# Two heads' attention scores as a pair of matmuls on the two halves of TensorE's rows, instead of one full-height matmul for each head

## The chip, the core and the metric

The kernel runs on one core of a Trainium2 chip. The metric is the device time of one execution in microseconds (us), the median of several runs. TensorE (PE) multiplies matrices and keeps its weights in a separate load (PEld), VectorE (DVE), ScalarE (ACT) and GpSimd (POOL) work on what it leaves in PSUM or on SBUF, and SyncE (SP) issues most of the DMAs.

## The reference

```python
xn = layernorm(x)                                   # x: 2048 x 576
qkv = (xn @ wqkv).reshape(B, S, 3, 32, 18)          # 32 heads of 18 numbers
scores = einsum("bhqd,bhkd->bhqk", q, k) * 18**-0.5
mask = (i - j >= 0) & (i - j < 256)                 # causal, a window of 256
p = softmax(where(mask, scores, -1e9))
s = einsum("bhqk,bhkd->bhqd", p, v).reshape(B, S, D) @ wo
z = gelu(xn @ w_in);  z1, z2 = z[:2304], layernorm(z[2304:])
g = w_sp @ z2 + b_sp                                # w_sp: 2048 x 2048
out = x + s * silu((z1 * g) @ w_out)
```

The change is in `scores` and in the row maxima that the softmax subtracts. Everything else stays as it is.

## The kernel before

Products are made in fp32r, each factor split into a high and a low part where precision asks for it. The kernel goes through these stages, told with the stretch of the profiled execution that they take: layernorm, q and k (stored to DRAM in `st_d` as high and low parts) and v (0 to 203 us); the z2 product (203 to 444 us, matmul line L688); a stage of heads, in which attention is computed and the z1 product (L460) is woven in as filler (444 to 940 us); then the large `w_sp` product in Strassen form (L1001), `wo` and `w_out` to the end.

**Attention.** The work is cut into 16 units: 4 heads and one half of the 2048 positions each. An SBUF tile `att` (a slot) holds two heads. A head's q takes 54 rows, high part, the same high part again, and low part, against k's low, high and high part, so that one matmul over 54 rows gives the whole product. Head 0 of a slot sits on rows 0 to 53, head 1 on rows 64 to 117. k of both heads shares the same columns, but q of the two heads stands in separate columns, and the other head's rows there are zero. A matmul for one head therefore reads all the rows of the slot, and the zeros take the other head out.

**Row maxima** (`row_max`, L398 on). For each head and each block of 128 queries a matmul `sp` (L409, 118 rows, 384 keys wide, 256 in the first two blocks) writes a PSUM tile of the pool `sps`, and DVE reduces it to a maximum in one custom instruction with an accumulator read behind it (L413). After 32 of these, a small transpose (`sp<-ident,mx`, L421) turns the maxima of the unit into rows, DVE splits them in two parts (L425, L426), and `put_max` (L428) sends them by two DMAs on POOL's queue into rows 126 and 127 of the slots, where k has ones. `row_max` is a generator. One `next` of it is a step: one matmul with its reduction, or one of three steps at the end (35 steps a unit).

**Scores for the softmax** (`scores`, L523 on). For each block of 128 keys and each head a matmul `tps` (L539, all 128 rows, so that the maximum is subtracted inside the product, 384 or 256 queries wide) writes a PSUM tile of the pool `tps`, and ACT takes the exponential out of it (L543). After four heads POOL masks the corners (L546, L549), and later `pv` (L552 on) multiplies by v: groups of four matmuls `ops` (L562), one head in each 32 columns of TensorE.

**PSUM.** All eight banks are taken: two each for `mm` (z1, z2), `sp`, `tps` and `ops`. So the pools `sps` and `tps` have two tiles each, and a matmul that wants a tile waits until DVE or ACT is done with the tile two before it.

**Order.** The stages with attention are under a manual schedule: the instructions of PE, DVE, ACT and POOL stand as the Python loops issue them, so the order of the code is the order on each engine. In the z2 stage two steps of `row_max` go into each group of 14 matmuls over its last blocks, to get ahead of the heads (L684 to L691; `RMN + LEAD` steps in all). In the heads' stage the loop over `items` (L745 on) takes one head of one key block at a time: its `tps` matmul, then alternately a filler (`fill`, one z1 matmul) and a step of `row_max` as they fall due, and every four key blocks a burst of `pv`. Loads of a head (`load_head`, four DMAs) and of v are issued at fixed items, two units ahead.

Of the kernel before, what the change touches and what calls it, by code (L numbers as in the profile page):

```python
# [9 lines left out]
F32 = mybir.dt.float32  # L10
# [6 lines left out]
P = 128  # L17
# [15 lines left out]
SLOT = 2 * HS + HS + 256  # L33
# [6 lines left out]
RMN = 35  # L40
LEAD = 16
# [4 lines left out]
DR = 118  # L46
LOAD_AT = (1, 9, 16, 24)
# [16 lines left out]
def kernel(  # L64
# [47 lines left out]
    dve.reduce_sum(low, ident[:64, :64].rearrange("p (a n b) -> p n a b", n=2, b=16)[:, 1], axis=mybir.AxisListType.XY)  # L112
# [133 lines left out]
    with ExitStack() as early:  # L246
# [103 lines left out]
        with ExitStack() as ph:  # L350
# [3 lines left out]
            def clear(i):  # L354
                eng = (dve, pool)[i % 2]
                eng.memset(f32(slots[i][:, 0:2 * HS]), 0.0)
                eng.memset(f32(slots[i][:, 2 * HS:]), 1.0)
# [3 lines left out]
            def q_of(u, j):  # L361
                t = slots[(2 * u + j // 2) % NSLOT]
                return t[:, (j % 2) * HS:(j % 2 + 1) * HS]

            def k_of(u, j):
                return slots[(2 * u + j // 2) % NSLOT][:, 2 * HS:]

            def load_head(u, j):
                g, half = UNITS[u]
                q0 = half * HS  # L370
                k0, kn = (0, HS) if half == 0 else (HS - 256, HS + 256)
                h = 4 * g + j
                q, k = f32(q_of(u, j)), f32(k_of(u, j))
                b = 64 * (j % 2)
                qs, ks = st_d[0, :, h, q0:q0 + HS], st_d[1, :, h, k0:k0 + kn]
                sp.dma_start(q[b:b + 36, :], qs)
                sp.dma_start(k[b:b + 18, :kn], ks[18:36])
                sp.dma_start(q[b + 36:b + 54, :], qs[18:36])
                sp.dma_start(k[b + 18:b + 54, :kn], ks)
# [18 lines left out]
            def row_max(u):  # L398
# [3 lines left out]
                for j in range(4):  # L402
                    for i in range(8):
                        qb = 8 * half + i
                        w = 384 if qb >= 2 else 256
                        k0 = (max(qb - 2, 0) - base) * P
                        m0 = {0: 256, 1: 128}.get(qb, 0)
                        ps = sps.tile([P, 384], F32, name="sp")
                        pe.matmul(ps[:, :w], q_of(u, j)[:DR, i * P:(i + 1) * P], k_of(u, j)[:DR, k0:k0 + w],  # L409
                                  start=True, stop=True)  # L410
                        spend(MM * w / 512 + 20)
                        junk = aa.tile([P, 384], mybir.dt.bfloat16, name="junk")
                        dve.tensor_tensor_reduce(out=junk[:, :w], in0=ps[:, :w], in1=band[:, m0:m0 + w], scale=1.0,  # L413
                                                 scalar=-3.0e38, op0=ALU.add, op1=ALU.max,
                                                 accum_out=mx[:, j // 2, 0, j % 2, i:i + 1])
                        yield
                dve.tensor_copy(mx[:, :, 1], mx[:, :, 0])
# [3 lines left out]
                pe.transpose(pt[:64, :P], mx.rearrange("p a n b i -> p (a n b i)"), ident)  # L421
# [6 lines left out]
                def put_max(n):  # L428
                    t = slots[(2 * u + n) % NSLOT]
                    pool.dma_start(f32(t[126:128, 0:2 * HS]), f32(m[32 * n:32 * n + 32, :]))  # L430

                for n in range(2):
                    after(1000 + 600 * n, partial(put_max, n))
# [89 lines left out]
            def scores(u, kb, qa, qz, j):  # L523
# [3 lines left out]
                if j == 0:  # L527
# [7 lines left out]
                if n == 1:  # L535
                    a = qa - 1 if qa > lo else qa
                m = max(n, 2)
                ps = tps.tile([P, 384], F32, name="tps")
                pe.matmul(ps[:, :m * P], k_of(u, j)[:, (kb - base) * P:(kb - base + 1) * P],  # L539
                          q_of(u, j)[:, (a - lo) * P:(a - lo + m) * P], start=True, stop=True)  # L540
                spend(MM * m / 4 + 20)
                d0 = (qa - kb) * P
                act.activation(pt[:, j, d0:d0 + n * P], ps[:, (qa - a) * P:(qa - a + n) * P], AF.Exp, scale=scale)  # L543
                if j == 3:
# [173 lines left out]
            with ExitStack() as heads:  # L718
# [22 lines left out]
                for u in range(NU):  # L741
# [3 lines left out]
                    items = [(s, j) for s in steps for j in range(4)]  # L745
                    heads_at = {LOAD_AT[i]: (u + 2, i) for i in range(4) if u or i > 1}
                    have, want = done, (total - TAIL) * WEIGHT[u]
                    for t, (s, j) in enumerate(items):
# [3 lines left out]
                        if u == NU - 1 and t == 4:  # L752
# [17 lines left out]
                        while z >= 0.5 or r >= 0.5:  # L770
                            if z >= 0.5:
                                fill(1)
                                z -= 1
                            if r >= 0.5:
                                next(stream, None)
                                maxed += 1
                                r -= 1
                            if z < 1.5 and j == 3 and len(todo) >= (PVN if u < NU - 1 else 2):
                                burst()
                        if j == 3 and len(todo) >= (PVN if u < NU - 1 else 2):  # L780
                            burst()
                        if j == 3:
                            todo.append((u, *s))
                        if j == 1:
                            extra(1)
                        if t == 12 and u + 1 < NU:
                            load_v(u + 1)
                        if u == NU - 1 and t >= 8 and prep:
                            prep.pop(0)()
# [426 lines left out]
```

## Time and profile before

| | |
|---|---|
| median of 3 runs | 1939.77 us (1939.09 to 1940.27) |
| the profiled execution | 1937.71 us |
| its span, first to last instruction | 1936.0 us |
| granted TensorE clock, mean | 0.999 |
| PE matmul busy | 1910.9 us (99%) |
| DVE / ACT / POOL busy | 1076.2 (56%) / 892.4 (46%) / 288.1 us (15%) |
| the same in 446 to 940 us (494 us) | PE 493.0, DVE 299.2, ACT 311.3, POOL 171.1 us |

A line such as `650.28 0.33 PE L539 MATMUL tps<-att 128*128 128x384 f32 x1` says: at 650.28 us of the span, 0.33 us long, on PE, from line 539 of the kernel, tile `tps` from tile `att`, 128 rows by 128 columns of weights, 384 numbers streamed. Matmuls are pipelined: what one costs is the distance from its start to the start of the next, and not its length, which holds the time until its result has landed. What stands in square brackets is how long the engine sat idle before and who released it; "issue" there means that the engine waited for nothing that the profile shows.

### The profile page before, as it was taken

How to read it: one execution, taken by the hardware profiler on the slowest of the kernel's cores; microseconds unless marked ns; L12 is line 12 of the kernel's file. 1: busy time of each engine (PE TensorE's matmuls, PEld its weight loads, DVE VectorE, ACT ScalarE, POOL GpSimd, SP SyncE). 2: the span in 40 equal slices, each digit the busy share in tenths (PEclk: the TensorE clock that was granted, in tenths of full speed). 3: DMA queues.
4: the chain of work that ended last, by engine and by line, in shares of the span. 5: the costliest groups of instructions: out<-in, count | busy, mean ns of one | idle time of the engine just before them, and what ended most of it. 6: DMA issues, size and time to landing. Idle time of an engine off the chain costs nothing.

```text
span 1936.0 us, 30625 instructions
## 1 busy us (share of the span) xinstructions
PE 1910.9 (99%) x11095; PEld 1658.4 (86%) x11095; DVE 1076.2 (56%) x2294; ACT 892.4 (46%) x1663; POOL 288.1 (15%) x388
## 2 busy tenths in 40 slices
PE   7999999999999999999999999999999999999998
PEld 5889999998777787877788888888888878999998
DVE  6522243367666666663277777666776877533322
ACT  4212222216665666666575566545655345422211
POOL 1101243433332333333100000000000000000000
PEclk9999999999999999999999999999999999999999
DMA  7655578975554655544576687757867778954442
GB/s 218 193 136 164 193 256 274 286 239 137 133 145 117 151 140 135 132 132 130 181 252 212 208 269 243 236 165 235 280 217 238 236 243 279 304 182 145 147 139 66
DMA packets 218510, 376.88 MB, mean 195 GB/s; under 512 B 40383, under 2 KB 117055, under 8 KB 217591
## 3 DMA queue, kind: packets, MB, share of 16 engines
q1 hardware_dynamic: 214135, 367.75, 61.9%
q10 hardware_dynamic: 2304, 5.09, 0.7%
q0 software_dynamic: 1920, 2.09, 0.4%
q8 instruction: 87, 1.43, 0.3%
q14 instruction: 64, 0.52, 0.1%
HBM read 261.76 MB, written 117.81 MB: 196 GB/s over the span
## 4 chain that ended last, share of the span: by engine, by line
PE 95%; DMA 3%; DVE 1%; ACT 1%; issue 0%; SPq 0%; DVEq 0%; ACTq 0%
PE acc L1001 34%; PE mm L460 12%; PE mm L688 12%; PE po L1143 12%; PE mm L326 6%; PE tps L539 5%; PE sp L409 5%; PE ops L562 4%; PE vps L478 3%; PE wops L1100 2%; DMA s_d<-so 1%; DMA spr<-sc_d 1%; DMA wraw<-in_wqkv_dram 1%; PE tpt L309 0%; DMA xr<-in_x_dram 0%
## 5 line engine op out<-in xcount | busy, mean ns | idle before, releaser
L1001 PE MATMUL acc<-sph,zh 128*128 128x512 f32 x1008 | 392.8, 390 | 3.8 <-ACT sph L229 3.7
L1001 PE MATMUL acc<-spl,zh 128*128 128x512 f32 x1008 | 393.0, 390 | 0.8 <-DVE spl L229 0.8
L1001 PE MATMUL acc<-sph,zl 128*128 128x512 f32 x1008 | 392.7, 390 | 0.0
L413 DVE CUSTOM_DVE_ANT_0 junk<-sp,band 128x384 bf16<-128x384 f32 (+1 forms) x512 | 273.7, 540 | 142.8 <-PE sp L409 138.6
L543 ACT ACTIVATE pt<-tps 128x384 f32<-128x384 f32 (+2 forms) x576 | 247.9, 439 | 125.4 <-PE tps L539 115.8
L460 PE MATMUL mm<-b,z1wh 128*128 128x512 f32 x648 | 250.2, 398 | 0.0
L229 DVE TENSOR_TENSOR spl<-spr,sph 128x1024 fp32r<-128x1024 f32 x166 | 203.2, 1224 | 65.7 <-ACT sph L229 64.8
L1001 PEld LDWEIGHTS acc<-sph,zh 128*128 128x128 f32 x1008 | 189.5, 188 | 44.1 <-ACT sph L229 4.1
L1001 PEld LDWEIGHTS acc<-spl,zh 128*128 128x128 f32 x1008 | 189.6, 188 | 40.7 <-DVE spl L229 1.1
L1001 PEld LDWEIGHTS acc<-sph,zl 128*128 128x128 f32 x1008 | 189.6, 188 | 39.2
L688 PE MATMUL mm<-z2wh,b 128*128 128x384 f32 x720 | 193.1, 335 | 0.0
L539 PE MATMUL tps<-att 128*128 128x384 f32 (+1 forms) x576 | 188.1, 327 | 0.9 <-ACT pt L543 0.8
L229 ACT ACTIVATE zh<-b 128x384 fp32r<-128x384 f32 x144 | 75.8, 527 | 241.2 <-PE acc L1001 241.1
L229 ACT ACTIVATE sph<-spr 128x1024 fp32r<-128x1024 f32 x166 | 174.2, 1049 | 20.2 <-DMA spr<-sc_d 10.4
L409 PE MATMUL sp<-att 118*128 118x384 f32 (+1 forms) x512 | 171.9, 336 | 0.0
L1143 PE MATMUL po<-b,yh 128*128 128x288 f32 x896 | 155.8, 296 | 0.0
L229 DVE TENSOR_TENSOR zl<-b,zh 128x384 fp32r<-128x384 f32 x144 | 80.1, 556 | 114.0 <-ACT zh L229 113.9
L460 PE MATMUL mm<-b,z1wl 128*128 128x512 f32 x360 | 142.7, 396 | 0.0
L460 PEld LDWEIGHTS mm<-b,z1wh 128*128 128x128 f32 x648 | 122.2, 189 | 23.9 <-issue 4.9
L688 PE MATMUL mm<-z2wl,b 128*128 128x384 f32 x400 | 134.0, 335 | 0.0
L539 PEld LDWEIGHTS tps<-att 128*128 128x128 f32 x576 | 109.1, 189 | 26.7 <-issue 7.6
L1143 PEld LDWEIGHTS po<-b,yh 128*128 128x128 f32 x896 | 131.9, 189 | 0.0
(159 smaller groups left out, 2793.9 us busy)
## 6 DMA issues: line engine op xcount, KB each, us to landing
spr<-sc_d SPq DMA_DIRECT2D x96, 512.0 KB
spr<-in_w_sp_dram SPq DMA_DIRECT2D x72, 512.0 KB
zr<-z_d SPq DMA_DIRECT2D x136, 192.0 KB
st_d<-qkhl SPq DMA_DIRECT2D x72, 256.0 KB
z_d<-zt SPq DMA_DIRECT2D x96, 192.0 KB
z_d<-z1o SPq DMA_DIRECT2D x72, 256.0 KB
z1t<-z_d SPq DMA_DIRECT2D x72, 256.0 KB
yr<-y_d SPq DMA_DIRECT2D x48, 384.0 KB
```

The source lines that it names most:

```text
L229: job()
L326: pe.matmul(ps, w, r, start=n == 0, stop=n == len(pl) - 1)
L409: pe.matmul(ps[:, :w], q_of(u, j)[:DR, i * P:(i + 1) * P], k_of(u, j)[:DR, k0:k0 + w], start=True, stop=True)
L413: dve.tensor_tensor_reduce(out=junk[:, :w], in0=ps[:, :w], in1=band[:, m0:m0 + w], scale=1.0, scalar=-3.0e38, op0=ALU.add, op1=ALU.max, ac ...
L460: pe.matmul(ps, w, r, start=n == 0, stop=n == len(pl) - 1)
L478: pe.matmul(ps[:, i, :288], r, w[:, i * 288:(i + 1) * 288], start=n == 0, stop=n == len(pl) - 1)
L539: pe.matmul(ps[:, :m * P], k_of(u, j)[:, (kb - base) * P:(kb - base + 1) * P], q_of(u, j)[:, (a - lo) * P:(a - lo + m) * P], start=True, s ...
L543: act.activation(pt[:, j, d0:d0 + n * P], ps[:, (qa - a) * P:(qa - a + n) * P], AF.Exp, scale=scale)
L562: pe.matmul(o_ps[c][32 * j:32 * j + 32, (lo - 4 * c) * P:(hi - 4 * c + 1) * P], vgs[u][:, kb - k0, j * VW:j * VW + 32], pt[:, j, (lo - kb) ...
L688: pe.matmul(ps[:, :ZW], r, wt, start=n == 0, stop=n == len(pl) - 1)
L1001: pe.matmul(acc[j], z[:, ps], w[:, cs], start=s == i == 0 and n in OPENS, stop=s == 7 and i == 2, skip_group_check=True)
L1143: pe.matmul(po[i][:, a, :288], y[:, i * P:(i + 1) * P], w[:, a * 288:(a + 1) * 288], start=f == 0 and m == 0, stop=f == NF - 1 and m == 2)
```

## The change

q of both heads now shares columns, as k does, each on its own rows, and there are no zeros. A matmul reads only its own head's rows: 54 (`DR`) for the maxima, on rows 0 to 53 or 64 to 117, and 56 (`DS`) for the scores, on rows 0 to 55 or 64 to 119. The two rows behind a head's own hold its maxima (k has ones there), so `put_max` runs four times a unit, one DMA for each head. In the built program these 512 `sp` and 576 `tps` matmuls are placed on a tile of 64 rows by 128 columns of TensorE, at row 0 or row 64, where before they took all 128 by 128. All other matmuls keep their placement: 128 by 128, except `ops` (128 by 32) and the 15 small transposes of the maxima (128 by 64).

The two heads of a slot are issued one right after the other: `row_max` writes both tiles of `sps` and then reduces both, and `scores` writes both tiles of `tps` and then takes both exponentials. A step of `row_max` is now such a pair (19 steps a unit instead of 35, `LEAD` 8 instead of 16), and an item of the heads' loop is a pair (288 instead of 576). In that loop the steps of `row_max` that are due now come right behind the scores, ahead of the filler, and no longer alternate with it.

```diff
-SLOT = 2 * HS + HS + 256
+SLOT = HS + HS + 256
-RMN = 35
-LEAD = 16
+RMN = 19
+LEAD = 8
-DR = 118
-LOAD_AT = (1, 9, 16, 24)
+DR = 54
+DS = 56
+LOAD_AT = (1, 5, 8, 12)
...
-                eng.memset(f32(slots[i][:, 0:2 * HS]), 0.0)
-                eng.memset(f32(slots[i][:, 2 * HS:]), 1.0)
+                eng.memset(f32(slots[i][:, HS:]), 1.0)
...
-            def q_of(u, j):
-                t = slots[(2 * u + j // 2) % NSLOT]
-                return t[:, (j % 2) * HS:(j % 2 + 1) * HS]
+            def q_of(u, j, rows=64):
+                b = 64 * (j % 2)
+                return slots[(2 * u + j // 2) % NSLOT][b:b + rows, :HS]
...
-                        ps = sps.tile([P, 384], F32, name="sp")
-                        pe.matmul(ps[:, :w], q_of(u, j)[:DR, i * P:(i + 1) * P], k_of(u, j)[:DR, k0:k0 + w],
-                                  start=True, stop=True)
+                        pair = []
+                        for j in (2 * a, 2 * a + 1):
+                            pair.append(sps.tile([P, 384], F32, name="sp"))
+                            pe.matmul(pair[-1][:, :w], q_of(u, j, DR)[:, i * P:(i + 1) * P],
+                                      k_of(u, j, DR)[:, k0:k0 + w], start=True, stop=True)
...
+                        for b in range(2):
+                            junk = aa.tile([P, 384], mybir.dt.bfloat16, name="junk")
+                            dve.tensor_tensor_reduce(out=junk[:, :w], in0=pair[b][:, :w], in1=band[:, m0:m0 + w],
...
-                    pool.dma_start(f32(t[126:128, 0:2 * HS]), f32(m[32 * n:32 * n + 32, :]))
-                for n in range(2):
+                    pool.dma_start(f32(q_of(u, n)[DR:DS]), f32(m[16 * n:16 * n + 16, :]))
+                for n in range(4):
...
-                ps = tps.tile([P, 384], F32, name="tps")
-                pe.matmul(ps[:, :m * P], k_of(u, j)[:, (kb - base) * P:(kb - base + 1) * P],
-                          q_of(u, j)[:, (a - lo) * P:(a - lo + m) * P], start=True, stop=True)
+                js = (2 * pair, 2 * pair + 1)
+                pss = [tps.tile([P, 384], F32, name="tps") for _ in js]
+                for ps, j in zip(pss, js):
+                    pe.matmul(ps[:, :m * P], k_of(u, j, DS)[:, (kb - base) * P:(kb - base + 1) * P],
+                              q_of(u, j, DS)[:, (a - lo) * P:(a - lo + m) * P], start=True, stop=True)
...
-                act.activation(pt[:, j, d0:d0 + n * P], ps[:, (qa - a) * P:(qa - a + n) * P], AF.Exp, scale=scale)
+                for ps, j in zip(pss, js):
+                    act.activation(pt[:, j, d0:d0 + n * P], ps[:, (qa - a) * P:(qa - a + n) * P], AF.Exp, scale=scale)
...
-                    items = [(s, j) for s in steps for j in range(4)]
+                    items = [(s, j) for s in steps for j in range(2)]
...
-                        while z >= 0.5 or r >= 0.5:
-                            if z >= 0.5:
-                                fill(1)
-                                z -= 1
-                            if r >= 0.5:
-                                next(stream, None)
-                                maxed += 1
-                                r -= 1
+                        while r >= 0.5:
+                            next(stream, None)
+                            maxed += 1
+                            r -= 1
+                        while z >= 0.5:
+                            fill(1)
+                            z -= 1
```

On PE, in the middle of a unit of the heads' stage, this stood before (`mm<-b,z1wh` and `z1wl` are the filler):

```order
L539 MATMUL tps<-att_1201 128x384
L460 MATMUL mm<-b_98,z1wl 128x512
L409 MATMUL sp<-att_4223 128x384
L460 MATMUL mm<-b_98,z1wh 128x512
L539 MATMUL tps<-att_1201 128x384
L460 MATMUL mm<-b_101,z1wh 128x512
L409 MATMUL sp<-att_4223 128x384
L460 MATMUL mm<-b_98,z1wl 128x512
```

At such a place there now stands this, with one place where two steps of `row_max` fall due at once (a `sp` pair right behind a `sp` pair):

```order
L543 MATMUL tps<-att_1199 128x384 x2
L411 MATMUL sp<-att_1775 128x256 x2
L411 MATMUL sp<-att_1775 128x384 x2
L462 MATMUL mm<-b_101,z1wh 128x512
L462 MATMUL mm<-b_99,z1wl 128x512
L462 MATMUL mm<-b_102,z1wh 128x512
L462 MATMUL mm<-b_102,z1wl 128x512
L543 MATMUL tps<-att_1200 128x384 x2
L411 MATMUL sp<-att_1775 128x384 x2
L462 MATMUL mm<-b_97,z1wh 128x512
```

Four single matmuls, each between fillers, became one run of four and then three or four fillers. A run of half-height matmuls without anything else between is called a visit here. Over the whole program there are 311 visits: 201 with a `tps` pair and a `sp` pair, 71 with a `tps` pair alone, 16 with a `tps` pair and two `sp` pairs, and 23 with a `sp` pair alone. The last kind is in the z2 stage, where PE had this before, a `sp` after every 5 and 9 matmuls of z2 and over 25 of its blocks:

```order
L409 MATMUL sp<-att_1199 128x384
L688 MATMUL mm<-z2wl,b_98 128x384
L688 MATMUL mm<-z2wh,b_98 128x384
L688 MATMUL mm<-z2wh,b_101 128x384
L688 MATMUL mm<-z2wl,b_98 128x384
L688 MATMUL mm<-z2wh,b_99 128x384
L409 MATMUL sp<-att_1199 128x384
```

It now has pairs at the same distances, over the last 13 blocks:

```order
L411 MATMUL sp<-att_1199 128x384 x2
L693 MATMUL mm<-z2wl,b_97 128x384
L693 MATMUL mm<-z2wh,b_98 128x384
L693 MATMUL mm<-z2wh,b_101 128x384
L693 MATMUL mm<-z2wl,b_98 128x384
L693 MATMUL mm<-z2wh,b_99 128x384
L411 MATMUL sp<-att_1199 128x384 x2
```

The number of matmuls of each kind is the same in both programs. What moved is which ones stand beside each other, and how many of PSUM's tiles a run needs at once.

More of the change, by code (lines that the diff above doesn't have):

```diff
@@ L111 @@
     low = const.tile([64, 1], F32, name="low")
-    dve.reduce_sum(low, ident[:64, :64].rearrange("p (a n b) -> p n a b", n=2, b=16)[:, 1], axis=mybir.AxisListType.XY)
+    dve.reduce_sum(low, ident[:64, :64].rearrange("p (a n b) -> p n a b", n=2, b=8)[:, 1], axis=mybir.AxisListType.XY)
     dve.tensor_scalar(low, low, -1.0, None, ALU.mult)
@@ L401, in row_max @@
                 mx = aa.tile([P, 2, 2, 2, 8], F32, name="mx")
-                for j in range(4):
+                for a in range(2):
                     for i in range(8):
@@ L407, in row_max @@
                         m0 = {0: 256, 1: 128}.get(qb, 0)
-                        ps = sps.tile([P, 384], F32, name="sp")
-                        pe.matmul(ps[:, :w], q_of(u, j)[:DR, i * P:(i + 1) * P], k_of(u, j)[:DR, k0:k0 + w],
-                                  start=True, stop=True)
-                        spend(MM * w / 512 + 20)
[L412 to L415, printed above, removed]
+                        pair = []
[3 more added lines that the diff above has]
+                                      k_of(u, j, DR)[:, k0:k0 + w], start=True, stop=True)
+                        spend(MM * w / 512 + 20)
+                        for b in range(2):
+                            junk = aa.tile([P, 384], mybir.dt.bfloat16, name="junk")
+                            dve.tensor_tensor_reduce(out=junk[:, :w], in0=pair[b][:, :w], in1=band[:, m0:m0 + w],
+                                                     scale=1.0, scalar=-3.0e38, op0=ALU.add, op1=ALU.max,
+                                                     accum_out=mx[:, a, b, 0, i:i + 1])
                         yield
-                dve.tensor_copy(mx[:, :, 1], mx[:, :, 0])
+                dve.tensor_copy(mx[:, :, :, 1], mx[:, :, :, 0])
                 yield
@@ L420, in row_max @@
                 pt = sps.tile([P, 384], F32, name="sp")
-                pe.transpose(pt[:64, :P], mx.rearrange("p a n b i -> p (a n b i)"), ident)
+                pe.transpose(pt[:64, :P], mx.rearrange("p a b n i -> p (a b n i)"), ident)
                 spend(110)
@@ L521, in steps_of, with scores @@
                 return [(kb, max(kb, lo), min(kb + 2, hi)) for kb in range(max(lo - 2, 0), hi + 1)]
-            def scores(u, kb, qa, qz, j):
+            def scores(u, kb, qa, qz, pair):
                 half = UNITS[u][1]
@@ L526, in scores @@
                 base = 0 if half == 0 else 6
-                if j == 0:
+                if pair == 0:
                     own = u == NU - 1 or len(seen) % NPT < 3
@@ L751 @@
                             load_head(*heads_at[t])
-                        if u == NU - 1 and t == 4:
+                        if u == NU - 1 and t == 2:
                             spare.close()
```

32 lines of the change are left out of this document (16 added, 16 removed).

## The prediction

> **What bounds the kernel now.** I read the engines' busy time first, then the stretch that holds the heads, then the chain that ended last in it.
>
> ```profile
> PE 1910.9 (99%) x11095; PEld 1658.4 (86%) x11095; DVE 1076.2 (56%) x2294; ACT 892.4 (46%) x1663; POOL 288.1 (15%) x388
> 446.00:940.00 494.00, 493.00 (x3430) 386.83 (x3429) 299.21 (x1044) 311.33 (x733) 171.10 (x270) 1.00 0.53 135
> by line: PE mm L460 45.8%; PE tps L539 19.4%; PE ops L562 16.8%; PE sp L409 16.6%; PE sp L421 0.5%; ACT pt L543 0.3%; DVE mx L417 0.1%; ACT z1o L463 0.1%; DVE junk L413 0.1%; ACT sph L789 0.1%; issue 0.1%; ACT zh L789 0.1%; ACT z1wh L496 0.
> by line: PE mm L688 86.1%; PE sp L409 10.7%; PE mm L460 3.3%; PE sp L421 0.2%
> PEld tps L539 <- ACT pt L543: 7.2, 21, 0.9
> PEld sp L409 <- DVE mx L413: 3.1, 14, 0.3
> ```
>
> The second line is 446 to 940 us: PE is busy for 493 of 494 us, DVE and ACT for about 60%. The third is the chain there, the fourth the chain in 375 to 446 us, the end of z2. PE's own work is the time, and whatever leaves PE's queue shortens it. The matmuls in question hold (19.4 + 16.6)% of 494 = 177.8 us and 10.7% of 71 = 7.6 us, together 185.4 us; the last two rows say that 10.3 us of it are waits for ACT and DVE, so 175.1 us are matmuls. The steady rhythm shows what each costs, and how soon its reader starts:
>
> ```profile
> 650.28 0.33 PE L539 MATMUL tps<-att 128*128 128x384 f32 x1
> 650.45 0.39 PE L460 MATMUL mm<-b,z1wh 128*128 128x512 f32 x1
> 650.45 0.19 PEld L409 LDWEIGHTS sp<-att 118*128 118x128 f32 x1
> 650.68 0.34 PE L409 MATMUL sp<-att 118*128 118x384 f32 x1
> 650.71 0.49 ACT L543 ACTIVATE pt<-tps 128x384 f32<-128x384 f32 x1 [0.60 <-PE tps L539]
> 650.86 0.40 PE L460 MATMUL mm<-b,z1wh 128*128 128x512 f32 x1
> 651.06 0.56 DVE L413 CUSTOM_DVE_ANT_0 junk<-sp,band 128x384 bf16<-128x384 f32 x1 [0.25 <-PE sp L409]
> ```
>
> Start to start, a score matmul of 384 takes 0.17 to 0.18 us and a filler 0.23 us. Weight loads (0.19 us) are hidden under the matmul ahead. ACT starts 0.43 us after its matmul, DVE 0.38 us.
>
> **The change, part by part.** First, *two heads at once*. The trace has no matmuls on half the rows, but it has `ops`, four at once on quarters of the columns:
>
> ```profile
> L562 PE MATMUL ops<-pt,vg 128*32 128x384 f32 (+2 forms) x1408 | 86.0, 387 | 0.0
> ```
>
> 1408 of 387 ns would be 545 us one after another; they take 86 us. I take it that halves of the rows run side by side as quarters of the columns do. Then half of 175.1 us goes, 87.6 us, less about 4 us for the second starts (544 pairs, under 0.01 us each, an estimate). With the old waits out too, the matmuls shrink from 185.4 to 91.6 us: **-94 us**, and new waits are counted below. The other bound is 0, if they run in turn.
>
> Second, *going to half-height and back*. PE switches its layout 311 times more each way. Nearest is the visit to `ops`, entered from a filler and left for a score matmul:
>
> ```profile
> 759.97 0.40 PE L460 MATMUL mm<-b,z1wh 128*128 128x512 f32 x1
> 760.30 0.32 PE L562 MATMUL ops<-pt,vg 128*32 128x128 f32 x4
> ...
> 761.62 0.83 PE L562 MATMUL ops<-pt,vg 128*32 128x384 f32 x8
> ...
> 761.94 0.51 PE L562 MATMUL ops<-pt,vg 128*32 128x384 f32 x4
> 762.38 0.45 PE L539 MATMUL tps<-att 128*128 128x384 f32 x1
> 762.66 0.40 PE L460 MATMUL mm<-b,z1wl 128*128 128x512 f32 x1
> 655.49 0.19 PEld L539 LDWEIGHTS tps<-att 128*128 128x128 f32 x1 [0.20 <-issue]
> ```
>
> Going in, the filler takes 0.33 instead of 0.23 us: +0.10. Coming out, eight matmuls are two groups of four, the second (shown again by itself) 0.32 us behind the first, and `tps` follows 0.44 us later instead of 0.32: +0.12, of which 0.02 are the four starts of a group. Then that `tps` takes 0.28 instead of 0.17: +0.11. The last row says why: the weight load does not run ahead across the switch, it starts with its matmul after 0.20 us of nothing. So out costs about 0.20, in 0.10 with weights 32 columns wide. The pairs' weights are 128 wide, which cost 0.11 in the open; I put a quarter of that into the 0.10 and add the rest: 0.17 to 0.18. A visit thus costs 0.37 us, and 311 of them **+115 us**. The other bound is this place, the transpose of the maxima on half the columns:
>
> ```profile
> 546.50 0.40 PE L460 MATMUL mm<-b,z1wh 128*128 128x512 f32 x1
> 546.73 0.27 PE L421 MATMUL sp<-ident,mx 128*64 128x128 f32 x1
> 546.76 0.48 PE L460 MATMUL mm<-b,z1wl 128*128 128x512 f32 x1
> 547.07 0.34 PE L539 MATMUL tps<-att 128*128 128x384 f32 x1
> 546.58 0.11 PEld L421 LDWEIGHTS sp<-ident,mx 128*64 128x64 f32 x1
> ```
>
> The filler ahead keeps its 0.23 us, the load runs ahead, and the switch costs nothing that the rows show. I take the dearer row: `ops` is the only place where neighbouring matmuls lie at several positions of the array, as the pairs will. The upper bound is 0.48 us, if the two weight loads of a pair go one after the other (0.11 more).
>
> [...]
>
> Third, *the waits that pairs bring*. A pair takes both tiles of its pool, so its second matmul waits until both readers of the pair before are done.
>
> ```profile
> 646.33 0.56 DVE L413 CUSTOM_DVE_ANT_0 junk<-sp,band 128x384 bf16<-128x384 f32 x1 [0.20 <-PE sp L409]
> 646.94 0.19 PEld L409 LDWEIGHTS sp<-att 118*128 118x128 f32 x1 [0.21 <-DVE mx L413]
> 642.55 1.58 ACT L543 ACTIVATE pt<-tps 128x384 f32<-128x384 f32 x3
> L463 ACT ACTIVATE z1o<-mm 128x512 f32<-128x512 f32 x72 | 42.8, 596 | 10.0 <-PE mm L460 6.2 <-issue 2.8
> L698 DVE BATCH_NORM_STATS2 st<-zt 128x6 f32<-128x384 f32 x96 | 53.7, 559 | 139.1 <-ACT zt L697 139.1
> ```
>
> A waiting load starts 0.05 us after the reduction's end (646.89 to 646.94). So DVE gives a pair back 0.38 + 2 x 0.56 + 0.05 = 1.55 us after its start; ACT after 0.43 + 2 x 0.53 + 0.05 = 1.54 us (three exponentials take 1.58). A visit comes round in 0.37 + 2 x 0.18 + 3.3 x 0.23 = 1.49 us: 3.3 fillers, since 1008 less 12 ahead and some 56 behind are spread over 288 items. So readers and PE are nearly level, and what disturbs them is paid:
> - 16 visits have two `sp` pairs in a row. The second waits out the whole 1.55 us instead of its 0.18: 1.37 each, 22 us. Everything behind it in PE's queue waits too.
> - ACT's eviction of z1 (0.60 us, 72 times) falls between exponentials. I take 0.15 us each (between 0, where a burst of `ops` follows, and 0.60): 11 us.
> - 71 visits have a `tps` pair alone, round in 1.31 us, short of ACT's 1.54 by 0.23. After a wait the next visit has some slack and a third of them is narrower (less ACT), so 0.08 each: 6 us.
> - In z2 every second pair follows after five matmuls, 5 x 0.17 + 0.55 = 1.40 us against 1.55, with the 0.56 of the statistics between for some: 0.3 each, 12 times: 4 us.
>
> Sum **+43 us** (bounds 20 and 80).
>
> Fourth, *what costs nothing*.
>
> ```profile
> L430 POOL DMA_DIRECT2D att<-mhl x30 | 18.5, 617 | 15.2 <-DVE mhl L426 14.3 <-DVE z1wl L496 0.9
> L356 POOL MEMSET att<- 128x2048 f32 x3 | 5.4, 1812 | 23.2 <-ACT pt L543 18.8 <-PE mm L688 4.4
> ```
>
> 30 more maxima DMAs are 18.5 us on POOL, which is busy 171 of 494 us; they are issued eight items, over 11 us, ahead of their use, and the masks queued behind them wait 0.6 us at most. If that cover went, the first scores of 15 units would wait a few us each. The zero fills that go (1.8 us each) and the rest of the initial work lie beside PE's z2 work. Head loads keep their number and sizes on SP.
>
> **Sum.** 1937.7 (the profiled execution) - 94 + 115 + 43 = 2002 us; its own distance to the median of the runs is 2.1 us, which gives 2004. I forecast 2003 us, slower.
>
> **The rivals.** *The switch is free.* If half rows behave as the transpose does, 115 us fall away, and a visit comes round in 1.12 us. The readers then set the pace: on 201 visits half the missing 0.43 us, less the eighth that follows a burst, 38 us; lone `tps` pairs 71 x 0.25 = 18; the doubles 22; z1's evictions 14; z2 4: 96 us, and the sum is 1942 with the 2.1 us. These waits are worked out as if each fell alone. Waits for ACT and DVE in one visit overlap, which I put at a fifth to a half: 1939.8 - 94 + 48 to 77 = 1894 to 1923, faster, or about level if they don't overlap. The point that decides: switch and waits together below 94/311 = 0.30 us a visit. For it speaks the transpose's rows, against it `ops`.
>
> *The pairs run in turn*, so the change doesn't do what it says: 175 us stay, 115 come, waits fall to some 25, since visits are longer: 1939.8 - 10 + 115 + 25 = 2070. Against it speak the four at once of `ops`.
>
> *A cheap switch*, half of 0.37: 1939.8 - 94 + 57 + 60 = 1963, slower still.
>
> **How the numbers follow.** My case gets 0.55 (its own range 1970 to 2040), the cheap switch 0.10, the free one 0.27 (faster 0.19, same 0.03, slower 0.05), pairs in turn 0.08. Faster by over 0.2% (4 us, what a measurement of this kernel can tell) is 0.19 and 0.01 out of my case, were its switch and waits far too high: 0.20; same is 0.03 and 0.02 out of my case: 0.05; slower is the rest, 0.75. The range leaves out the pairs in turn and the lower part of the free switch, together some 0.19: 1915 to 2040.
>
> **What would show it.** Right: in the changed trace the two matmuls of a pair start within 0.02 us; the filler ahead of a visit takes 0.3 us or more; the first filler behind it is late by 0.2 us and long; idle time of PEld put down to "issue" grows by some 60 us or more; and where two `sp` pairs follow each other PE sits 1.3 us. Wrong: fillers of 0.23 us on both sides of a visit, with loads running ahead (the free switch); second matmuls 0.17 us behind the first (pairs in turn); or PE idle on ACT or DVE for far more than 43 us.

## The result, and the profile after

The changed kernel takes 2019.41 us (median of 4 runs, 2018.54 to 2020.98); the kernel before takes 1939.43 us beside it (4 runs, 1938.03 to 1940.27). The ratio is 1.0415, with an interval of 1.04 to 1.0429: slower by 4%. The profiled execution took 2019.28 us (before 1937.71), its span 2017.6 us, and its mean granted clock 0.992 (before 0.999).

From the page after: the busy times, and the granted clock in 40 slices of 50 us.

```profile
PE 1978.5 (98%) x11095; PEld 1578.6 (78%) x11095; DVE 1048.9 (52%) x2291; ACT 873.3 (43%) x1663; POOL 296.4 (15%) x415
PEclk9999999997999999999999999999999999999999
```

PE is still the engine that is always busy, now for 68 us longer with the same 11095 matmuls, while DVE and ACT do slightly less. One slice, 454 to 504 us, ran at a clock of 0.7. Nearly all of the loss is in z2 and the heads: from z2's first matmul to the first matmul of the `w_sp` product (L1006 after) it is 202.28 to 1027.22 us, 824.9 us, where before it was 745.0 us (202.40 to 947.39). That is +79.9 us of the +81.6 us between the two profiled executions.

The windows view of the heads' stage after, with the columns of the row for 446 to 940 us before, and behind it two parts of the stretch in which the clock fell:

```profile
446.00:1020.00 574.00, 561.48 (x3480) 315.91 (x3480) 283.79 (x1068) 295.58 (x738) 183.25 (x296) 0.98 0.46 117
440.00:500.00 60.00, 53.27 (x236) 32.31 (x235) 32.47 (x120) 22.27 (x52) 14.80 (x22) 0.80 0.31 87
460.00:480.00 20.00, 17.39 (x50) 9.59 (x50) 8.78 (x39) 9.77 (x21) 3.66 (x6) 0.57 0.51 143
```

PE is no longer busy throughout: it is idle for 12.5 us in 574 (1 us in 494 before), and 6.7 us in the 60 between 440 and 500 us alone. The weight loads are the larger sign: nearly as many loads (3480, before 3429) are 316 us instead of 387, since two loads of a pair now overlap in the records.

A visit in the steady rhythm after, PE and then PE's weight loads (x2 is a pair, in one row):

```profile
673.22 0.40 PE L462 MATMUL mm<-b,z1wh 128*128 128x512 f32 x1
673.54 0.45 PE L543 MATMUL tps<-att 56*128 56x384 f32 x2
673.83 0.34 PE L411 MATMUL sp<-att 54*128 54x384 f32 x2
674.09 0.50 PE L462 MATMUL mm<-b,z1wh 128*128 128x512 f32 x1
674.43 0.39 PE L462 MATMUL mm<-b,z1wl 128*128 128x512 f32 x1
674.66 0.40 PE L462 MATMUL mm<-b,z1wh 128*128 128x512 f32 x1
```

```profile
673.54 0.19 PEld L543 LDWEIGHTS tps<-att 56*128 56x128 f32 x2 [0.36 <-ACT pt L548]
673.65 0.19 PEld L411 LDWEIGHTS sp<-att 54*128 54x128 f32 x2
674.09 0.19 PEld L462 LDWEIGHTS mm<-b,z1wh 128*128 128x128 f32 x1 [0.25 <-issue]
674.20 0.19 PEld L462 LDWEIGHTS mm<-b,z1wl 128*128 128x128 f32 x1
```

Read the starts. The filler ahead keeps 0.32 us instead of 0.23 before the pair starts. The `tps` pair holds PE for 0.29 us, the `sp` pair for 0.26, the first filler behind for 0.34 instead of 0.23, the next 0.23 again. The loads of `tps` and of the first filler start together with their matmul, at 673.54 and at 674.09: at a change of height no load runs ahead here, so part of it lies in the open. The load of the `sp` pair at 673.65 does run under the `tps` pair, on the same rows, 0.18 us ahead of its matmul. Over the whole stage the second matmul of a pair starts 0.004 us behind the first, in the mean, wherever it does not wait (395 of 544 pairs).

The waits view after, for 400 to 1030 us (total, times, longest):

```profile
PEld mm L462 <- issue: 68.9, 299, 0.6
PEld tps L543 <- ACT pt L548: 64.5, 169, 3.2
PEld tps L543 <- issue: 34.2, 98, 0.7
PEld sp L411 <- DVE mx L416: 21.4, 36, 3.2
PE sp L411 <- DVE mx L416: 12.1, 17, 2.9
```

The first row is the fillers behind visits, 0.23 us each, 299 times; before there were 18 such idle times. The second row must be read with care: ACT is named as what ended last before the load, but such loads start after 0.36 us of idle time (the median of the 169), and so do the 98 of the third row, under "issue", which waited for nothing that the profile shows (0.36 too).

Two single waits stand out, at the seam between z2 and the heads. The first, on PE, DVE and POOL after, and the same DVE work before:

```profile
441.09 0.34 PE L693 MATMUL mm<-z2wh,b 128*128 128x384 f32 x1
444.34 1.03 PE L411 MATMUL sp<-att 54*128 54x384 f32 x2 [2.91 <-DVE mx L416]
...
440.19 3.58 DVE L711 TENSOR_TENSOR z1wl<-z1raw,z1wh 128x256 fp32r<-128x256 f32 x3
...
440.59 1.29 POOL L620 TENSOR_TENSOR a<-a,a 128x512 f32<-128x512 f32 x1
441.96 1.33 POOL L621 TENSOR_TENSOR a<-a,a 128x512 f32<-128x512 f32 x1
```

```profile
436.44 0.95 DVE L706 TENSOR_TENSOR z1wl<-z1raw,z1wh 128x256 fp32r<-128x256 f32 x3
```

Three splits of z1's weights (two of 256 columns, one of 128, merged in one row), 0.95 us before, took 3.58 us beside two POOL sums; the reductions stood behind them, and the next `sp` pair waited 2.91 us. In all the traces of this case together, twelve splits of 256 columns run beside such a sum, in six kernels, and take 1.1 to 2.0 us each; the 125 that run beside nothing on POOL take 0.41 to 0.43 us. The second wait is ACT's: it loads its table twice, and a `tps` pair waits 2.78 us for an exponential:

```profile
462.09 1.07 PE L543 MATMUL tps<-att 56*128 56x384 f32 x2 [2.78 <-ACT pt L548]
...
458.29 1.28 ACT L123 ACT_TABLE_LOAD   x1
460.25 1.28 ACT L548 ACT_TABLE_LOAD   x1
```

About the end of each wait the granted clock falls to a half, from 444.6 to 448.0 and from 461.6 to 478.7 us. A third stretch, 492.3 to 495.8 us, comes behind a place with two `sp` pairs, where PE made no start for 0.90 us. That is 24 us at half clock in this stage.

### The profile page after: what moved, and what is told of

It is laid out like the page before. It is cut to its first block, busy times and chain, and to the rows that moved or that the text cites. A ratio compares the mean times of both kernels' runs of the same rounds, so it can differ in the third digit from the quotient of the medians.

```text
span 2017.6 us, 30688 instructions
## 1 busy us (share of the span) xinstructions
PE 1978.5 (98%) x11095; PEld 1578.6 (78%) x11095; DVE 1048.9 (52%) x2291; ACT 873.3 (43%) x1663; POOL 296.4 (15%) x415
## 4 chain that ended last, share of the span: by engine, by line
PE 94%; DMA 3%; DVE 1%; ACT 1%; issue 0%; SPq 0%; DVEq 0%; ACTq 0%
PE acc L1006 33%; PE mm L462 15%; PE mm L693 12%; PE po L1148 11%; PE mm L327 6%; PE tps L543 5%; PE ops L567 4%; PE sp L411 4%; PE vps L480 3%; PE wops L1105 1%; DMA s_d<-so 1%; DMA spr<-sc_d 1%; DMA wraw<-in_wqkv_dram 1%; DVE junk L416 0%; PE tpt L310 0%
## 5 line engine op out<-in xcount | busy, mean ns | idle before, releaser
L1006 PE MATMUL acc<-sph,zh 128*128 128x512 f32 x1008 | 393.6, 391 | 3.9 <-ACT sph L230 3.7
L1006 PE MATMUL acc<-spl,zh 128*128 128x512 f32 x1008 | 393.8, 391 | 0.8 <-DVE spl L230 0.8
L1006 PE MATMUL acc<-sph,zl 128*128 128x512 f32 x1008 | 393.5, 390 | 0.0
L416 DVE CUSTOM_DVE_ANT_0 junk<-sp,band 128x384 bf16<-128x384 f32 (+1 forms) x512 | 256.1, 537 | 194.9 <-PE sp L411 194.4
L548 ACT ACTIVATE pt<-tps 128x384 f32<-128x384 f32 (+2 forms) x576 | 220.6, 436 | 189.0 <-PE tps L543 187.5
L1006 PEld LDWEIGHTS acc<-sph,zh 128*128 128x128 f32 x1008 | 190.0, 188 | 44.1 <-ACT sph L230 4.2
L1006 PEld LDWEIGHTS acc<-spl,zh 128*128 128x128 f32 x1008 | 190.0, 188 | 40.6 <-DVE spl L230 1.2
L1006 PEld LDWEIGHTS acc<-sph,zl 128*128 128x128 f32 x1008 | 190.0, 188 | 39.4
L462 PEld LDWEIGHTS mm<-b,z1wh 128*128 128x128 f32 x648 | 118.1, 191 | 58.0 <-issue 45.6
L462 PE MATMUL mm<-b,z1wl 128*128 128x512 f32 x360 | 156.3, 434 | 0.0
L543 PEld LDWEIGHTS tps<-att 56*128 56x128 f32 x576 | 60.0, 185 | 106.5 <-ACT pt L548 64.5
L703 DVE BATCH_NORM_STATS2 st<-zt 128x6 f32<-128x384 f32 x96 | 53.8, 560 | 162.9 <-ACT zt L702 162.9
L551 POOL TENSOR_SCALAR_AFFINE_SELECT pt<-pt 128x512 f32<-128x512 f32 x128 | 85.4, 667 | 339.4 <-ACT pt L548 339.4
L693 PEld LDWEIGHTS mm<-z2wh,b 128*128 128x128 f32 x720 | 131.6, 189 | 2.3 <-issue 1.9
```

Source lines behind the costliest of these rows:

```text
L416: dve.tensor_tensor_reduce(out=junk[:, :w], in0=pair[b][:, :w], in1=band[:, m0:m0 + w], scale=1.0, scalar=-3.0e38, op0=ALU.add, op1=ALU.ma ...
L462: pe.matmul(ps, w, r, start=n == 0, stop=n == len(pl) - 1)
L543: pe.matmul(ps[:, :m * P], k_of(u, j, DS)[:, (kb - base) * P:(kb - base + 1) * P], q_of(u, j, DS)[:, (a - lo) * P:(a - lo + m) * P], start ...
L551: pool.affine_select(out=pt[:, :, 0:P], in_=pt[:, :, 0:P], pattern=[[0, 4], [1, P]], compare_op=ALU.is_ge, fill=0.0, base=0, channel_multi ...
L693: pe.matmul(ps[:, :ZW], r, wt, start=n == 0, stop=n == len(pl) - 1)
L1006: pe.matmul(acc[j], z[:, ps], w[:, cs], start=s == i == 0 and n in OPENS, stop=s == 7 and i == 2, skip_group_check=True)
```

## The experiments

**Pairs, but at full height** (`e1_pairs_full`). The order, the pairs and the waits of the changed kernel, on the layout of before: q of the two heads in separate columns with zeros beside it, 118 and 128 rows for every matmul. Neither the side-by-side run nor the switch is left.

```diff
-DR = 54
-DS = 56
+DR = 118
+DS = 128
...
-                b = 64 * (j % 2)
-                return slots[(2 * u + j // 2) % NSLOT][b:b + rows, :HS]
+                c = HS * (j % 2)
+                return slots[(2 * u + j // 2) % NSLOT][:rows, c:c + HS]
```

> The changed kernel's order and pairs, with every score matmul at full height again (the layout with zeros of before). It has the pairs' waits without the side-by-side run and without the switch. My theory (the switch between full and half height costs about 0.39 us a visit, 311 times, some 120 us, against 94 saved; the waits and the stretch at half clock are the other 50): 1939 - 10 + 50 = 1980 us, 1965 to 1995, so well below the changed kernel's 2019. The rival that the pairs' waits on two PSUM tiles are the loss and the switch is nearly free: these waits would be some 170 us in the changed kernel, and at least 80 remain here where a visit is 0.35 us longer: 2020 us or more.

Measured: 1972.19 us (1970.51 to 1974.07), ratio 1.0172 (1.0155 to 1.0189). The new order with its waits alone costs 33.5 us over before, of which about 3 us are two stretches of half clock of 3.4 us each; with the 10 us of waits that were there before, pairs wait some 41 us. Both stalls at the seam are in this kernel too (2.70 and 3.17 us from start to start, at 439.04 and 455.24 us), and its clock falls at 443.2 and 460.2 us, within 2 us of their ends. The other 47 us of the loss come with half height: its switches less what the pairs save, and the longer half clock, 24 us instead of 7, which is worth 9 us at most.

**Half height in single matmuls** (`e2_half_row0`, `e3_half_row64`). In the kernel before, half of the 512 `sp` matmuls, those of one head of each slot, read 54 rows only: rows 0 to 53 in one kernel, rows 64 to 117 in the other. Each is a visit of its own between two fillers, with nothing gained from it.

```diff
+                        rows = slice(64 * 0, 64 * 0 + 54) if j % 2 == 0 else slice(0, DR)
-                        pe.matmul(ps[:, :w], q_of(u, j)[:DR, i * P:(i + 1) * P], k_of(u, j)[:DR, k0:k0 + w],
+                        pe.matmul(ps[:, :w], q_of(u, j)[rows, i * P:(i + 1) * P], k_of(u, j)[rows, k0:k0 + w],
```

The second kernel has `slice(64 * 1, 64 * 1 + 54) if j % 2 == 1`.

> The kernel before, with the maxima matmuls of head 0 of each slot (256 of 512) on rows 0 to 53 alone, so on a tile of 64 rows by 128 columns at row 0; order, pairs and everything else as before, and nothing runs side by side. My theory: 256 switches each way at 0.39 us, 100 us: 2039 us. The rival that a tile at row and column 0 needs no switch, as the small transpose of the maxima at column 0 shows none: 1939 us.

> The same with the maxima matmuls of head 1 of each slot on rows 64 to 117, a tile at row 64. My theory: 2039 us, as at row 0. The rival that only a tile away from row 0 needs a switch: 2039 us here and 1939 us at row 0. If half height were free: 1939 us in both.

Measured: 2033.5 us, ratio 1.0486 (1.0465 to 1.0507), and 2034.62 us, ratio 1.0492 (1.0471 to 1.0513). That is +94.8 and +95.9 us, 0.370 and 0.375 us for each of 256 visits. The forecast's 0.37 is hit, and the place on the rows makes no difference. PE and its loads with rows 0 to 53:

```profile
653.12 0.39 PE L461 MATMUL mm<-b,z1wh 128*128 128x512 f32 x1
653.44 0.44 PE L410 MATMUL sp<-att 54*128 54x384 f32 x1
653.81 0.50 PE L461 MATMUL mm<-b,z1wh 128*128 128x512 f32 x1
654.15 0.34 PE L540 MATMUL tps<-att 128*128 128x384 f32 x1
...
653.44 0.18 PEld L410 LDWEIGHTS sp<-att 54*128 54x128 f32 x1 [0.31 <-issue]
653.81 0.19 PEld L461 LDWEIGHTS mm<-b,z1wh 128*128 128x128 f32 x1 [0.18 <-issue]
```

In four parts again: filler ahead 0.32 (+0.09), the half matmul 0.37 instead of 0.18 (+0.10 at its load, +0.09 going out), the filler behind 0.34 (+0.10). A change of height and back cost 0.37 us even for a tile at row 0, while in the change the second tile of a pair follows the first by 0.004 us. Of the four parts two (0.09 us each) are time in which the matmul ahead holds PE longer; the other two are loads in the open.

**Twice the visits** (`e4_two_visits`). The `tps` pair and the `sp` pair of an item no longer stand together: a filler goes between them, as in the loop before. 544 visits instead of 311, the pairs themselves unchanged.

```diff
-                        while r >= 0.5:
-                            next(stream, None)
-                            maxed += 1
-                            r -= 1
-                        while z >= 0.5:
-                            fill(1)
-                            z -= 1
+                        while z >= 0.5 or r >= 0.5:
+                            if z >= 0.5:
+                                fill(1)
+                                z -= 1
...
+                            if r >= 0.5:
+                                next(stream, None)
+                                maxed += 1
+                                r -= 1
```

> The changed kernel with one filler between the scores' pair and the maxima's pair, as the loop alternated before, so 544 visits instead of 311; no two pairs of maxima follow each other. My theory: 233 more visits at 0.39 us, 91 us, less up to 22 us of waits at the 16 doubled places: 2088 to 2110 us. The rival that the waits for readers are the loss: the pairs are spread over the fillers, so readers have more time, and it is below 2019 us.

Measured: 2120.19 us (2114.43 to 2125.94), ratio 1.0933 (1.0898 to 1.0969): +101 us over the change as it was made. 233 further visits at 0.39 us are 91 us. That leaves 10 for the rest, which is two things of opposite sign: shorter waits (the steps from one score matmul to the next of the same pool sum to 15 us, in the change to 36), and 113 us in which the clock was granted by half. The two runs lie far apart, 2114.43 us at a mean clock of 0.979 and 2125.94 us at 0.972; the trace is of the latter. Three stretches of this kernel, and a place in the second of them:

```profile
560.00:640.00 80.00, 79.28 (x424) 39.23 (x425) 37.82 (x149) 36.10 (x90) 24.13 (x39) 1.00 0.42 106
641.00:655.00 14.00, 13.73 (x91) 6.82 (x90) 6.18 (x25) 5.43 (x14) 6.16 (x9) 1.00 0.36 97
655.00:669.00 14.00, 14.00 (x43) 6.07 (x47) 3.91 (x16) 3.23 (x9) 1.86 (x3) 0.52 0.19 50
```

```profile
652.34 0.49 PE L462 MATMUL mm<-b,z1wh 128*128 128x512 f32 x1
653.07 0.92 PE L411 MATMUL sp<-att 54*128 54x384 f32 x2 [0.23 <-DVE mx L416]
```

The step from 652.34 to 653.07, 0.73 us, is the longest between two starts in those 14 us, at full clock; in the next 14 us PE is busy all the time and gets through 43 matmuls instead of 91. So in this kernel the clock fell without any pause worth the name, and that puts the time above my range. The last 3.4 us ahead of the fall (as long as the shortest stretches of half clock in the change) were not like the rest, though: PE started 10 matmuls in them, and 14 in each of the two stretches of 3.4 us before.

**No doubled `sp` pairs** (`e5_no_doubles`). At most one `sp` pair goes into a visit, so that none waits for the reductions of the pair right ahead of it; 318 visits.

```diff
-                            next(stream, None)
+                            pairs = next(stream, 0) == 1
                             maxed += 1
                             r -= 1
+                            if pairs:
+                                break
```

> The changed kernel, in which no visit has two pairs of maxima (at most one a visit; the 16 doubled ones move to visits with scores alone). My theory: 16 waits of 1.37 us go, 22 us, nothing else: 1997 us, 1990 to 2005. If waits were hidden in something else (clock, or readers that stay behind), less: 2010 us or more.

Measured: 2004.11 us (2003.32 to 2005.84), ratio 1.0335 (1.0318 to 1.0352): 15.3 us less. This kernel pays for 7 more visits (2.7 us) and for a wait that the change doesn't have: 7 `sp` pairs now stand alone behind a transpose of the maxima, and their second matmul starts 0.82 us late, 5.7 us together, since DVE's split of the maxima (L429) holds its PSUM tile. So the doubles and what goes with them were worth about 24 us, of which up to 5 are the clock: half-clock time fell as well, from 24 to 13.7 us. The steps between starts in the change give the waits of its 16 doubled places as 18 us, 1.14 each and not 1.37. Such a place in the change, at half clock:

```profile
465.56 0.41 PE L411 MATMUL sp<-att 54*128 54x256 f32 x2
466.50 1.03 PE L411 MATMUL sp<-att 54*128 54x384 f32 x2 [0.52 <-DVE mx L416]
```

**No doubles, and a quiet seam** (`e6_no_doubles_seam`). On top of the last, the pairs in z2 come four blocks earlier, and 26 fillers instead of 12 stand ahead of the first scores, so that neither stall at the seam can hold PE.

```diff
-HEAD = 12
+HEAD = 26
...
-                            if n in (4, 9) and pc * NS + s >= 6 * NS - (RMN + LEAD) // 2:
+                            if n in (4, 9) and 6 * NS - 4 > pc * NS + s >= 6 * NS - 4 - (RMN + LEAD) // 2:
```

> The same, and the seam between z2 and the heads eased: the maxima ahead of the heads lie four z2 blocks earlier, so that none stands behind the split of the z1 weights on VectorE, and 26 instead of 12 fillers stand ahead of the first scores, so that the table load of ScalarE is covered. My theory: the two idle stretches of PE there (2.9 and 2.8 us) and the 24 us at half clock behind them (some 12 us) go as well: 2019 - 22 - 18 = 1979 us, 1970 to 1990. If the half clock has another cause it stays, and the time is about 1992 us. In neither case below the kernel before, since the switches alone cost more than the pairs save.

Measured: 1994.32 us (1993.78 to 1995.82), ratio 1.0284 (1.0269 to 1.03), 9.8 us less than without doubles alone. That is above my range, near the number that I had given to another cause of the half clock; but the trace speaks against that reading: the half clock is gone from the stage. 440 to 500 us in this kernel:

```profile
440.00:500.00 60.00, 59.78 (x342) 38.76 (x345) 33.92 (x132) 33.42 (x77) 16.05 (x27) 1.00 0.50 133
```

342 matmuls where the change had 236 in the same 60 us. In its waits view, 400 to 1010 us, the reductions (L416) have all but gone, the 7 waits for the maxima's split (L429) stand, and ACT's row does too:

```profile
PEld tps L543 <- ACT pt L548: 66.5, 182, 0.7
PEld sp L411 <- DVE mx L416: 0.9, 4, 0.3
PEld sp L411 <- DVE mhl L429: 4.5, 7, 0.6
PE sp L411 <- DVE mhl L429: 3.0, 7, 0.4
```

The seam and its clock were thus worth 10 us on top of the last kernel, where I had put them at 18, with 24 us of half clock where that kernel had 13.7. The 7 extra visits and their waits, 8 us, were in no sum.

**A short reduction** (`e7_short_max`). The change, with each reduction over 128 columns only; the maxima are those of a third of the window.

```diff
-                            dve.tensor_tensor_reduce(out=junk[:, :w], in0=pair[b][:, :w], in1=band[:, m0:m0 + w],
+                            dve.tensor_tensor_reduce(out=junk[:, :P], in0=pair[b][:, min(qb, 2) * P:(min(qb, 2) + 1) * P], in1=band[:, 256:384],
```

> The changed kernel with the reduction of a maximum over 128 of its 384 columns alone, which leaves out two thirds of the maxima's work on VectorE (the softmax then subtracts another number). VectorE gives a pair back after about 0.9 us instead of 1.55. My theory: only the waits for VectorE shrink, at the 16 doubled places by 10 us and in z2 by a few, and perhaps the half clock: 1992 to 2010 us. The rival that waits for readers, VectorE's among them, are the loss: 1960 us or less.

Measured: 2000.8 us, ratio 1.0317 (1.0296 to 1.0337): 18.6 us less. The group of the reductions shows what was taken away (min, median and max in ns, where the page after has a mean of 537):

```profile
L416 DVE CUSTOM_DVE_ANT_0 junk<-sp,band x512: 223/291/295, 405.5 to 940.4; 128x128 bf16<-128x128 f32 x171
```

That is in the range of my theory: a DVE of nearly twice the speed on this work gives back under a quarter of the loss, and half-clock time fell with it, from 24 to 17 us.

**Pairs on the same rows** (`e8_pairs_in_turn`). Both matmuls of a pair read the even head's rows, to have them run in turn; the odd heads' own scores are left out.

```diff
-                            pe.matmul(pair[-1][:, :w], q_of(u, j, DR)[:, i * P:(i + 1) * P],
+                            pe.matmul(pair[-1][:, :w], q_of(u, 2 * a, DR)[:, i * P:(i + 1) * P],
...
-                    pe.matmul(ps[:, :m * P], k_of(u, j, DS)[:, (kb - base) * P:(kb - base + 1) * P],
+                    pe.matmul(ps[:, :m * P], k_of(u, 2 * pair, DS)[:, (kb - base) * P:(kb - base + 1) * P],
...
```

> The changed kernel with both matmuls of a pair on the even head's rows, so that they can't run side by side; the visits, their switches and all other work stay. It leaves out the odd heads' own scores (they get those of the head beside them). My theory: the 89 us that the pairs save come back, and of some 55 us of waits and half clock about 20 go, since visits are longer: 2085 us, 2070 to 2100. The rival that side by side saves little, and that the changed kernel's pairs are bound by something else: 2019 to 2035 us.

Measured: 2106.5 us, ratio 1.0864 (1.0842 to 1.0886), +87 us over the change and somewhat above my range. A visit of this kernel:

```profile
687.22 0.62 PE L543 MATMUL tps<-att 56*128 56x384 f32 x2
687.68 0.51 PE L411 MATMUL sp<-att 54*128 54x384 f32 x2
688.12 0.50 PE L462 MATMUL mm<-b,z1wh 128*128 128x512 f32 x1
```

From `tps` to the filler it is 0.90 us; the change has 0.55 (673.54 to 674.09). The 0.35 is two matmuls of 0.17 to 0.18 us: that is what running side by side saves in a visit with both pairs. Over the stage the steps to second matmuls grew by 108 us, the other steps inside visits shrank by 36 us (weight loads going under the longer runs would explain it, which was not shown), and the fillers, in 78.5 us of half clock (24 in the change), cost the rest.

**One exponential for both heads** (`e9_one_exp_per_pair`). The kernel with the quiet seam, with the two `tps` tiles as one of two banks and one ACT instruction for both, against ACT's 66.5 us in its waits.

```diff
-                pss = [tps.tile([P, 384], F32, name="tps") for _ in js]
+                two = tps.tile([P, 2, 512], F32, name="tps", bufs=1)
+                pss = [two[:, b] for b in range(2)]
...
-                for ps, j in zip(pss, js):
-                    act.activation(pt[:, j, d0:d0 + n * P], ps[:, (qa - a) * P:(qa - a + n) * P], AF.Exp, scale=scale)
+                act.activation(pt[:, js[0]:js[1] + 1, d0:d0 + n * P], two[:, :, (qa - a) * P:(qa - a + n) * P],
+                               AF.Exp, scale=scale)
```

> The kernel without doubled maxima and with the eased seam, and on top one exponential for both heads of a pair (one PSUM tile of two banks), so ScalarE gives a pair back about 0.2 us earlier. My theory: PE loses some 10 us to ScalarE there, what the waits view puts at 66 us is mostly time in which PE still streams or switches: 1988 us, 1983 to 1994. The rival that the 66 us are lost time: 1960 us or less. It is also the best I have of this design; it stays above the kernel before, 1939, because 318 switches at 0.39 us are 124 us against some 96 saved.

Measured: 1995.21 us (1994.48 to 1995.56), ratio 1.0289 (1.0271 to 1.0306): no gain over 1994.32, and a miss. Its row in the waits view, 446 to 1000 us:

```profile
PEld tps L544 <- ACT pt L548: 67.3, 167, 1.0
```

The second matmuls' waits for ACT fell from 7.1 to 0.9 us, summed over the steps between starts, and the fillers ahead of visits grew from 97.9 to 104.0: with one tile the first matmul waits for both heads. And the row still says 67 us, though ACT now takes 0.71 us for a pair instead of twice 0.44. So it is mostly time in which PE streams the filler and switches, as the visit at 673.54 had it.

No version here beats the kernel before; the best of this design, the one with the quiet seam, is 55 us slower.

## Why the prediction was right, by its steps

The direction, the size (2003 forecast, 2019 measured) and the mechanism held, and the signs that the prediction named came: starts 0.004 us apart, a filler of 0.32 us ahead of a visit, a late and long one behind it, PEld's idle time under "issue" up by some 90 us. Of the 16 us between, 6 belong to a switch that was priced a little low and about 10 to a clock that the sum took for granted; waits came out some 6 lower than forecast, and smaller things make up for it.

*Two heads at once, -94.* Right. The second matmul starts 0.004 us behind the first, and with pairs on one set of rows a visit is 0.35 us longer. Summed over the starts in the stage, the score matmuls and their old waits shrank by 96 us; less 2 for the second starts, that is the 94 of the forecast. The rival "in turn" is out: the kernel in which the pairs do run in turn takes 2106.5 us.

*Going to half height and back, +115.* Right in kind and near in size, by a reason that did not hold. Single visits cost 0.370 to 0.375 us. In the change the four parts sum to 0.39: filler ahead +0.09, the first pair's load +0.10, out +0.09, the load of the filler behind +0.105. For 311 visits that is 121 us, 6 more than forecast. A visit whose scores are 256 columns wide costs about 0.05 more, since so short a run no longer covers the load of the `sp` pair: at 528.97 the load ends 0.07 us behind the start of its matmul (0.01 at 673.83), and the `sp` pair holds PE for 0.32 us instead of 0.27 (medians); 76 visits, some 4 us. Choosing the row of `ops` over that of the transpose decided the forecast, and it was the right row. But the reason given for it, that at `ops` neighbouring matmuls lie at several positions of the array, is not what counts: a single matmul at row 0, alone between two fillers, pays the same 0.37. That part of the choice was luck. The transpose's rows were also read too well: the filler behind it takes 0.31 us (546.76 to 547.07) instead of 0.23, and so it is, by about 0.08, with the matmul behind all 15 transposes of the kernel before. With the 0.03 that a transpose itself took there, that visit cost some 0.05 us and not nothing. Without the 121 us the changed kernel would stand near 1900, an estimate that leaves out the waits that shorter visits would bring. The rivals of a free and of a cheap switch are out by the two single-visit kernels, without any pair in them. That the two loads of a pair might go one after the other (0.48) is out as well, and the load of the `sp` pair at 673.65 stays hidden under a matmul on the same rows: from `tps` to the filler a visit with both pairs takes 0.55 us and one with a `tps` pair alone 0.37, so the `sp` pair adds a matmul's 0.18 and no load.

*Waits, +43.* Inside its bounds of 20 and 80, a little high, and as near as it is partly by luck: its parts were off both ways. The steps from one score matmul to the next of the same pool sum to 36 us (28 in `sps`, 7 in `tps`). Less the pairs' own time in them, some 5, that is 31 us of waits, and the two stalls at the seam are 6 more: 37. The 16 doubles were put at 22 us and gave 18. ACT's evictions and lone `tps` pairs were put at 17, and second matmuls waited 6 for ACT; ahead of visits the steps show no more. The pairs in z2 were put at 4 and gave 2. In place of what these lack stand the stalls, which the sum didn't have, and some 4 us of waits for DVE at single `sp` pairs. Full-height pairs had some 41 by another road.

*Nothing for maxima DMAs and fills.* Nothing in the trace speaks against it: POOL's maxima DMAs went from 18.5 to 33.9 us, and no `sp` or `tps` row of the waits view names POOL.

```profile
L432 POOL DMA_DIRECT2D att<-mhl x60 | 33.9, 570 | 9.9 <-DVE mhl L429 9.9
```

*What was missed: the clock.* 24 us at half clock cost 12 us at most; some of it lies in waits, so I put it at 10, an estimate. The forecast took the clock of before for granted. Put together: -94 + 121 + 4 (the narrow visits) + 37 + 10 = +78, against +79.9 in the stage.

What started the half clock is shown in part. Six kernels here have both stalls at the seam (the change, full-height pairs, twice the visits, no doubles, the short reduction, pairs in turn), and in all six the clock falls within 2 us of the end of each; in the two without the stalls, as in the kernel before, it does not fall in the stage at all. So the stalls start it, also without any change of tiling. Why it then stays for 3.4 us at full height and for up to 17.1 us in the change is open. So is the fall without a stall: it came five times with 544 visits, but also twice with the 311 visits of the pairs in turn and once in the change, there behind doubled places with a step of 0.8 to 0.9 us. Frequent switches are thus a candidate and not shown. That DVE's splits were slow because POOL summed beside them fits every split in the traces that ran beside such a sum, but no kernel was made in which the sums alone are moved.

## What to carry to other kernels

Running two small matmuls side by side saves the length of one; entering and leaving their tiling costs 0.37 to 0.39 us here, so in a kernel like this one a visit must hold more than two pairs of 384 columns (0.35 us saved) before it pays at all. Price a change of tiling from the matmuls on both sides of one that the trace has already, starts and weight loads both, and count visits, not pairs; where two places give different prices, a kernel with that one change in it settles which holds. A name in the waits view is only who ended last: ask whether the waiting instruction could have started any sooner.

## What the runs showed of the hardware

Between the full array and tiles of 64 rows, no weight load ran ahead in the visits shown (about 0.10 us in the open, each way), while within one tiling a load on the very rows of the running matmul ran 0.18 us ahead (673.65). The matmul ahead held PE 0.09 us longer on top, each way; there and back cost 0.370 us in all for a tile at row 0 and 0.375 us for one at row 64. At the transpose, on 128 by 64, the load ran 0.15 to 0.23 us ahead and the matmul ahead kept its time (0.18 us in z2, 0.23 to 0.24 in the heads), in the 9 of 15 that did not wait for DVE; only the matmul behind it held PE some 0.08 us longer. Why it is so much cheaper is open.

In the change the granted clock fell to a half about the end of two stalls of 3.25 and 3.18 us from start to start, and at full height about the end of stalls of 2.70 and 3.17 us. In the kernel with 544 visits it also fell, for 13.7 us at a time, with no such stall: in the 14 us ahead of one fall PE was busy for 13.73 and its matmuls never started more than 0.73 us apart, and in the 14 us behind it the clock was 0.52.

Three DVE splits, two on 256 columns and one on 128, took 3.58 us instead of 0.95 us while POOL added two tiles of 512 columns.
